# Fixing ScalarE's order, starting the weights' exponents a piece ahead, and moving loads to GpSimd's queue in a linear-attention and PReLU kernel

**Chip, cores, metric.** One core of one Trainium2 chip. Times are device microseconds (us) of one execution, the median of several runs; profile spans are a little shorter than the timed run (by about 2 us). All runs quoted were in the fast state and gave correct results.

Engines by their short names: PE (TensorE, matrix products), DVE (VectorE), ACT (ScalarE), GpSimd (POOL in the profile), SP (SyncE, here only an issuer of transfers).

## The reference

Gated linear attention over 768 positions, then a two-layer network with a PReLU between, all in float32. The weights arrive as float64, that is as pairs of 32-bit words, and are converted on the chip.

```python
f = 1.0 / (1.0 + np.exp(-f_logit))                    # (B=4, H=8, S=768, D=48)
for t in range(S):
    state = f[:, :, t, :, None] * state + np.einsum('bhd,bhe->bhde', k[:, :, t], v[:, :, t])
    y[:, :, t] = np.einsum('bhd,bhde->bhe', q[:, :, t], state)
x = y.transpose(0, 2, 1, 3).reshape(B * S, H * D)      # 3072 x 384
h = x @ w_in                                           # 384 x 2048
out = (np.maximum(h, 0) + alpha * np.minimum(h, 0)) @ w_out   # 2048 x 384
```

## The kernel before

The work is cut into 12 steps (6 chunks of 128 positions times 2 pairs of batches). A step interleaves the attention of one chunk with the network of the chunk before it. Both are Python generators; a string per step says in which order their pieces are emitted: P or Q are the seven preparation pieces (of this or of the next chunk), S the attention products, n the twelve network pieces (eight `ph` pairs, four `po`), w and v one piece each of the conversion of `w_in` and `w_out`. The first four steps have strings of their own, for there the conversion competes with everything else.

```python
def load_weights(dst, src, name):                      # pieces w and v
    for n in [...]:
        raw = work.tile([128, WP, 2], I32, tag="raw", ..., bufs=4)
        nc.sync.dma_start(out=raw..., in_=src[:, n:n + WP].bitcast(I32))
        lo, hi = raw[:, :, 0], raw[:, :, 1]
        e = work.tile([128, WP], I32, tag="e", ...)    # the pool's two buffers
        nc.vector.tensor_scalar(e, hi, 0x7FF00000, None, ALU.bitwise_and)
        nc.scalar.activation(e, e, AF.Relu, bias=bias, scale=8.0)      # the exponent, on ACT
        m = work.tile([128, WP], U32, tag="m", ...)
        nc.vector.tensor_scalar(m, ...)                # four more DVE instructions;
        nc.vector.scalar_tensor_tensor(m, ...)
        nc.vector.scalar_tensor_tensor(e, hi, ..., e, ...)   # this one waits for ACT
        nc.vector.scalar_tensor_tensor(flat[:, n:n + WP], m, 2.0 ** -31, e.bitcast(F32), ...)
        yield
...
# attention, from the states on                          # last piece S
        yield
        for ...: nc.scalar.copy(A[...], ad[...])
        for ...: nc.scalar.copy(A[...], off[...])
        py = pair(f"py_{i}")
        ...                                             # products into py
        y = work.tile([128, U, HP, C], F32, tag="y", ..., bufs=1)
        for u in range(U):
            nc.scalar.copy(y[:, u]..., py[:, u])        # ACT
        for hd in range(H):                             # ten transfers y -> xT
            ...
            (nc.sync if hd % 2 else nc.scalar).dma_start(out=xT[...], in_=y[...])
        yield
...
# network, last piece n
        for u in range(U):
            nc.scalar.copy(o, po[u][:, 0:DM])           # ACT, waits for the end of po
            nc.sync.dma_start(out=out[t0:t0 + C], in_=o)
        yield
...
    first = (
        "P7 S w S w S w S w S w2",
        "n w n w n w n w n w n w n2 P7 S v S v S v S v2 S v n2 v3 n v3 n",
        "n P n P n P n P n P n P n P n S n S n S2 n S Q3 n",
        "n P n P n P n P S n2 S n2 S n S n S Q4 n Q3 n",
    )
    with tc.manual_schedule(engines={mybir.EngineType.PE, mybir.EngineType.DVE}):
        ...
```

`manual_schedule` makes the program's order the order of the engines it names; on the others the scheduler chooses.

Names in the views: a chunk's attention goes from f (decay, after the sigmoid), kr, fs, qd and us (preparation) by `raw`, `qu`, `ad`, `off` and A (weights within the chunk) and ksn and `pd` (turned keys and increments of the state) to py, y and its rearranged form xT. The network goes from xT by `ph` (xT times `w_in`), neg (its negative part) and g (the PReLU, with om = 1 - alpha) to `po` (g times `w_out`) and its copy o.

Of the kernel before, what the change touches and what calls it, by code (L numbers as in the profile page):

```python
# [8 lines left out]
F32 = mybir.dt.float32  # L9
I32 = mybir.dt.int32  # L10
U32 = mybir.dt.uint32
AF = mybir.ActivationFunctionType
ALU = mybir.AluOpType

C = 128
DB = 32
MASKED = (1, 0)

U = 2
CH = 64  # L20
NC2 = C // CH
NB = DB // 4
WP = 512
# [3 lines left out]
def kernel(  # L27
# [28 lines left out]
    nc = tc.nc  # L56
    B, NC, _, HP, _ = qT.shape
    DM = v.shape[-1]
# [9 lines left out]
    NJ = C // DB  # L68
# [6 lines left out]
    work = ctx.enter_context(tc.tile_pool(name="work", bufs=2))  # L75
# [3 lines left out]
    def pair(name):  # L79
        return psa.tile([128, 2, 512], F32, tag="pair", name=name)  # L80
# [6 lines left out]
    om = const.tile([128, NF], F32, tag="om", name="om")  # L87
# [2 lines left out]
    lvl = const.tile([128, 2, DB], F32, tag="lvl", name="lvl")  # L90
    nc.scalar.dma_start(out=lvl, in_=masks)
    nc.scalar.dma_start(out=om, in_=alpha)
    nc.scalar.activation(om, om, AF.Identity, bias=1.0, scale=-1.0)



# [9 lines left out]
    for m in range(1, NB):  # L106
        lo = UO[m] + (4 if m == 1 else 0)
        n = NB - m
# [16 lines left out]
    bias = const.tile([128, 1], F32, tag="bias", name="bias")  # L125
    nc.gpsimd.memset(bias, -896.0 * 2.0 ** 23)
    ad = const.tile([128, U, 2, HP, DB], F32, tag="ad", name="ad")
    nc.gpsimd.memset(ad, 0.0)
    A = const.tile([128, U, H, C], F32, tag="A", name="A")
    nc.gpsimd.memset(A, 0.0)  # L130

    def load_weights(dst, src, name):





        flat = dst.rearrange("p a n -> p (a n)")
        ks = NK if dst is w_in_sb else 1
        per = flat.shape[1] // ks  # L140
        for n in [k * per + j for j in range(0, per, WP) for k in range(ks)]:
            raw = work.tile([128, WP, 2], I32, tag="raw", name=f"{name}_raw{n}", bufs=4)
            nc.sync.dma_start(out=raw.rearrange("p n two -> p (n two)"),
                              in_=src[:, n:n + WP].bitcast(I32))
            lo, hi = raw[:, :, 0], raw[:, :, 1]

            e = work.tile([128, WP], I32, tag="e", name=f"{name}_e{n}")
            nc.vector.tensor_scalar(e, hi, 0x7FF00000, None, ALU.bitwise_and)
            nc.scalar.activation(e, e, AF.Relu, bias=bias, scale=8.0)

            m = work.tile([128, WP], U32, tag="m", name=f"{name}_m{n}")
            nc.vector.tensor_scalar(m, hi.bitcast(U32), 11, 0x80000000, ALU.logical_shift_left, ALU.bitwise_or)
            nc.vector.scalar_tensor_tensor(m, lo.bitcast(U32), 21, m, ALU.logical_shift_right, ALU.bitwise_or)
            nc.vector.scalar_tensor_tensor(e, hi, -0x80000000, e, ALU.bitwise_and, ALU.bitwise_or)
            nc.vector.scalar_tensor_tensor(flat[:, n:n + WP], m, 2.0 ** -31, e.bitcast(F32), ALU.mult, ALU.mult)  # L155
            yield

    def rows(par):
        return slice(64 * par, 64 * par + D)

    def quads(t):
        return t.rearrange("p (n r) -> p n r", r=4)

    def attention(bp, c, x):

        i = f"{bp}_{c}"
        b0 = U * bp

        def load(name, src, bufs=2):
            t = work.tile([128, W], F32, tag=name, name=f"{name}_{i}", bufs=bufs)  # L170
            nc.sync.dma_start(out=t.rearrange("p (u x) -> p u x", u=U),
                              in_=src[b0:b0 + U, c].rearrange("u p h t -> p u (h t)"))
            return t

        f = quads(load("f", fT))
        q = load("q", qT, 1)
        k = load("k", kT)


# [27 lines left out]
        for m in range(2, NB):  # L207
            n = NB - m
# [16 lines left out]

        vt = work.tile([128, U, DM + 16], F32, tag="v", name=f"v_{i}", bufs=1)
        nc.gpsimd.memset(vt[:, :, DM:DM + 16], 0.0)
        nc.sync.dma_start(out=vt[:, :, 0:DM], in_=v[b0:b0 + U, c].rearrange("u t d -> t u d"))


        q3 = work.tile([128, GC, 3, DB], F32, tag="q3", name=f"q3_{i}", bufs=1)
# [20 lines left out]
        for u in range(U):  # L252
# [24 lines left out]
            for m in range(1, NB):  # L277
                lo = UO[m] + (4 if m == 1 else 0)
                n = DB - 4 * m
# [5 lines left out]
        off = pair(f"off_{i}")  # L285
        for u in range(U):
            for hp in range(HP):
                for cc in range(NC2):
                    g = (u * HP + hp) * NC2 + cc
                    o = (u * HP + hp) * DB  # L290
                    for par in range(2):
                        r_ = rows(par)
                        nc.tensor.matmul(off[CH * cc:CH * cc + DB, par, o:o + DB],  # L293
                                         lhsT=kh[r_, g], rhs=q3[r_, g, 2], start=True, stop=True)


        pk = pair(f"pk_{i}")
# [4 lines left out]
        ksn = work.tile([128, U, HP * 128], F32, tag="ksn", name=f"ksn_{i}", bufs=1)  # L302
        for u in range(U):
            nc.scalar.copy(ksn[:, u], pk[:, u])
        yield
        pd = pair(f"pd_{i}")
        for u in range(U):
            for hp in range(HP):
                for cc in range(NC2):
                    for par in range(2):  # L310
                        o = (u * HP + hp) * D
                        hd = 2 * hp + par
                        s_ = slice(CH * cc, CH * cc + CH)
# [17 lines left out]
        yield  # L331


        for j in range(NJ):
            s_ = slice(DB * j, DB * (j + 1))
            nc.scalar.copy(A[s_, :, :, s_], ad[s_].rearrange("p u r h t -> p u (r h) t"))  # L336
        for cc in range(NC2):
            s_ = slice(CH * cc, CH * cc + DB)
            for par in range(2):
                nc.scalar.copy(A[s_, :, par * HP:(par + 1) * HP, CH * cc + DB:CH * (cc + 1)],  # L340
                               off[s_, par, 0:U * HP * DB].rearrange("p (u h t) -> p u h t", u=U, h=HP))


        py = pair(f"py_{i}")
        for u in range(U):
            for hp in range(HP):
# [5 lines left out]
        for cc in range(NC2):  # L352
            if states[cc] is None:
                continue
            for u in range(U):
                for hp in range(HP):
                    for par in range(2):
                        r_ = rows(par)
                        o = hp * C + cc * CH
                        nc.tensor.matmul(py[64 * par:64 * par + D, u, o:o + CH],  # L360
                                         lhsT=states[cc][r_, u * HP + hp], rhs=qs[r_, u, hp, cc, 0:CH],
                                         start=False, stop=True, skip_group_check=True)
        y = work.tile([128, U, HP, C], F32, tag="y", name=f"y_{i}", bufs=1)
        for u in range(U):
            nc.scalar.copy(y[:, u].rearrange("p h t -> p (h t)"), py[:, u])
        xT = x["T"] = work.tile([128, NK, T], F32, tag="xT", name=f"xT_{i}")
        for hd in range(H):
            d = hd * D
            while d < (hd + 1) * D:
                n = min((hd + 1) * D, (d // 128 + 1) * 128) - d  # L370
                p0 = 64 * (hd % 2) + d - hd * D
                (nc.sync if hd % 2 else nc.scalar).dma_start(
                    out=xT[d % 128:d % 128 + n, d // 128].rearrange("p (u t) -> p u t", u=U),
                    in_=y[p0:p0 + n, :, hd // 2])
# [3 lines left out]
    def network(bp, c, x):  # L378
# [38 lines left out]
    steps = [(bp, c) for c in range(NC) for bp in range(B // U)]  # L417
    state = [None] * (B // U)
    first = (
        "P7 S w S w S w S w S w2",  # L420
        "n w n w n w n w n w n w n2 P7 S v S v S v S v2 S v n2 v3 n v3 n",
        "n P n P n P n P n P n P n P n S n S n S2 n S Q3 n",
        "n P n P n P n P S n2 S n2 S n S n S Q4 n Q3 n",
    )
    usual = "S n Q n S n Q n S Q n S Q n Q n S Q2 n5"
    pieces = {"w": load_weights(w_in_sb, w_in, "w_in"), "v": load_weights(w_out_sb, w_out, "w_out")}

    def begin(n):
        if n >= len(steps):
            return None, None  # L430
        x = {}
        return attention(*steps[n], x), network(*steps[n], x)

    with tc.manual_schedule(engines={mybir.EngineType.PE, mybir.EngineType.DVE}):
        att, net = begin(0)
        before = None
        for n in range(len(steps) + 1):
            coming, after = begin(n + 1)
            on = pieces | {"P": att, "S": att, "n": before, "Q": coming}
            for key in (first[n] if n < len(first) else usual).split():  # L440
                for _ in range(int(key[1:] or 1)):
                    if on[key[0]] is not None:
                        next(on[key[0]])
            before, att, net = net, coming, after
# [55 lines left out]
```

## Time and profile before

| | before |
|---|---|
| time, median of the first 3 runs | 736.37 us (734.86 to 737.44) |
| span of the profile | 732.2 us |
| start of step 2 (first `ph` of its network) | 152.83 us |
| `ph` of step 3's network flows (runs on without a long pause) from | 209.28 us |
| start of step 4 (`raw`), from here 52.57 us a step, PE never idle | 266.39 us |

The prediction shows the slices, the stretches and DVE's waits. Here are PE's own waits in the whole span. The columns are microseconds in total, how many waits, the longest.

```profile
PE raw L259 <- DVE qd L193: 18.9, 2, 13.1
...
PE po L402 <- DVE w_out_sb L155: 4.7, 4, 1.2
PE ph L386 <- DMA xT<-y: 4.2, 2, 4.0
...
PE pd L314 <- ACT ksn L304: 2.3, 3, 1.0
```

The line to remember is `ph <- DMA xT<-y`: the network of a chunk cannot begin before the ten transfers that turn y into xT have landed. Before the change that costs PE 4.2 us, nearly all of it once, in step 0, where there is no other network to work on meanwhile.

### The profile page before, as it was taken

How to read it: one execution, taken by the hardware profiler on the slowest of the kernel's cores; microseconds unless marked ns; L12 is line 12 of the kernel's file. 1: busy time of each engine (PE TensorE's matmuls, PEld its weight loads, DVE VectorE, ACT ScalarE, POOL GpSimd, SP SyncE). 2: the span in 40 equal slices, each digit the busy share in tenths (PEclk: the TensorE clock that was granted, in tenths of full speed). 3: DMA queues.
4: the chain of work that ended last, by engine and by line, in shares of the span. 5: the costliest groups of instructions: out<-in, count | busy, mean ns of one | idle time of the engine just before them, and what ended most of it. 6: DMA issues, size and time to landing. Idle time of an engine off the chain costs nothing.

```text
span 732.2 us, 17405 instructions
## 1 busy us (share of the span) xinstructions
PE 654.6 (89%) x7712; PEld 488.7 (67%) x7712; DVE 446.5 (61%) x895; ACT 187.2 (26%) x327; POOL 8.9 (1%) x42
## 2 busy tenths in 40 slices
PE   1368436889998999999999999999999999999997
PEld 0357335467677668678678678588687687687774
DVE  5969698869639588548458368279088186250020
ACT  3243114222222225114015024043041041041110
POOL 4000000000000000000000000000000000000000
PEclk9989855999999999999999999999999999999999
DMA  9244215401121022112121022022021001000000
GB/s 337 90 135 145 80 32 183 148 22 30 60 94 59 5 91 89 45 27 87 41 78 55 22 81 64 10 82 74 11 70 45 22 4 44 22 3 22 22 0 22
DMA packets 31466, 46.77 MB, mean 64 GB/s; under 512 B 3744, under 2 KB 19104, under 8 KB 31392
## 3 DMA queue, kind: packets, MB, share of 16 engines
q1 hardware_dynamic: 25536, 43.26, 18.7%
q10 hardware_dynamic: 5856, 2.40, 1.4%
q8 instruction: 61, 1.00, 0.6%
q14 instruction: 13, 0.11, 0.0%
HBM read 36.22 MB, written 4.72 MB: 56 GB/s over the span
## 4 chain that ended last, share of the span: by engine, by line
PE 78%; DVE 17%; ACT 2%; issue 1%; DMA 1%; ACTq 1%; DVEq 0%
PE ph L386 31%; PE po L402 31%; PE py L349 4%; PE py L360 3%; PE raw L259 2%; PE qu L275 2%; DVE us L210 2%; PE pk L301 2%; DVE ad L280 2%; PE pd L314 2%; DVE g L394 2%; DVE ad L266 1%; PE off L293 1%; DVE qd L193 1%; DVE w_out_sb L155 1%
## 5 line engine op out<-in xcount | busy, mean ns | idle before, releaser
L386 PE MATMUL ph<-xT,w_in_sb 128*128 128x256 f32 x1152 | 267.6, 389 | 13.0 <-DVE w_in_sb L155 8.0
L402 PE MATMUL po<-w_out_sb,g 128*128 128x384 f32 x768 | 252.6, 488 | 4.7 <-DVE w_out_sb L155 4.7
L386 PEld LDWEIGHTS ph<-xT,w_in_sb 128*128 128x128 f32 x1152 | 218.6, 193 | 50.4 <-DVE w_in_sb L155 9.4
L402 PEld LDWEIGHTS po<-w_out_sb,g 128*128 128x128 f32 x768 | 144.7, 190 | 105.1 <-DVE w_out_sb L155 8.5
L394 DVE SCALAR_TENSOR_TENSOR g<-neg,om,ph 128x256 f32<-128x256 f32 x192 | 83.2, 475 | 95.3 <-ACT neg L391 95.3
L266 DVE COPY_PREDICATED ad<-mraw,raw 128x256 f32<-128x256 int32 x96 | 42.5, 443 | 124.8 <-PE raw L259 122.3
L391 ACT ACTIVATE neg<-ph 128x512 f32<-128x512 f32 x96 | 57.1, 595 | 160.3 <-PE ph L386 128.2
L259 PE MATMUL raw<-qd,k 48*32 48x128 f32 x1536 | 31.0, 297 | 30.4 <-DVE qd L193 18.9
L408 ACT COPY o<-po 128x384 f32<-128x384 f32 x24 | 11.4, 480 | 172.0 <-PE po L402 172.0
L280 DVE COPY_PREDICATED ad<-mquad,qu 128x224 f32<-128x224 int32 (+6 forms) x168 | 50.3, 300 | 7.4
L259 PEld LDWEIGHTS raw<-qd,k 48*32 48x32 f32 x1536 | 23.9, 114 | 40.1 <-issue 35.7
L210 DVE TENSOR_TENSOR us<-us,fs 128x768 f32<-128x768 f32 (+2 forms) x72 | 44.9, 624 | 2.1
L275 PE MATMUL qu<-us,k 48*32 48x116 f32 x1536 | 29.3, 288 | 13.0 <-DVE us L210 9.9
L336 ACT COPY A<-ad 32x512 f32<-32x512 f32 x48 | 29.6, 616 | 35.5 <-DVE ad L280 34.9
L275 PEld LDWEIGHTS qu<-us,k 48*32 48x32 f32 x1536 | 23.9, 114 | 15.3 <-issue 7.0
L349 PE MATMUL py<-A,v 128*64 128x128 f32 x384 | 27.0, 300 | 2.4 <-issue 1.2
L349 PEld LDWEIGHTS py<-A,v 128*64 128x64 f32 x384 | 23.9, 152 | 6.4 <-issue 5.1
L193 DVE TENSOR_TENSOR qd<-qd,f 128x768 f32<-128x768 f32 (+2 forms) x36 | 27.3, 759 | 0.8
L199 DVE TENSOR_TENSOR us<-qd,f 128x1024 f32<-128x1024 f32 x12 | 24.1, 2009 | 0.1
L360 PE MATMUL py<-q,state 48*48 48x64 f32 x704 | 22.9, 221 | 0.0
L360 PEld LDWEIGHTS py<-q,state 48*48 48x48 f32 x704 | 21.1, 123 | 2.4 <-issue 2.4
L180 ACT ACTIVATE f<-f 128x1024 f32<-128x1024 f32 x12 | 12.7, 1057 | 36.1 <-DMA f<-in_fT 36.1
(62 smaller groups left out, 365.0 us busy)
## 6 DMA issues: line engine op xcount, KB each, us to landing
f<-in_fT SPq DMA_DIRECT2D x12, 512.0 KB, 3.8
q<-in_qT SPq DMA_DIRECT2D x12, 512.0 KB, 5.0
k<-in_kT SPq DMA_DIRECT2D x12, 512.0 KB, 3.9
w_in_raw<-in_w_in SPq DMA_DIRECT2D x12, 512.0 KB, 3.8
w_out_raw<-in_w_out SPq DMA_DIRECT2D x12, 512.0 KB, 3.5
v<-in_v SPq DMA_DIRECT2D x12, 384.0 KB, 3.3
out<-o SPq DMA_DIRECT2D x24, 192.0 KB, 2.0
xT<-y SPq DMA_DIRECT2D x36, 48.0 KB, 2.0
```

The costliest lines, as they stand in the source:

```text
L193: nc.vector.tensor_tensor(quads(qdv[d])[:, :, d:4], quads(qdv[d - 1])[:, :, d:4], f[:, :, 1:5 - d], ALU.mult)
L210: nc.vector.tensor_tensor(us[:, :, UO[m]:UO[m] + 4 * n].rearrange("p g (i r) -> p g i r", r=4), us[:, :, skip:skip + 4 * n].rearrange("p g ...
L259: nc.tensor.matmul(raw[DB * j:DB * (j + 1), par, hp * C:(hp + 1) * C], lhsT=k[r_, g:g + DB], rhs=qd[r_, 0:4 * W].rearrange("p (d x) -> p d ...
L266: nc.vector.copy_predicated(adu, mraw[:, d].rearrange("p i r -> p (i r)").bitcast(I32).unsqueeze(1).broadcast_to((128, H, DB)), rv[:, :, d])
L275: nc.tensor.matmul(qu[DB * j:DB * (j + 1), par, hp * UW:(hp + 1) * UW], lhsT=k4[r_, g * DB:(g + 1) * DB], rhs=us[r_, g], start=True, stop= ...
L280: nc.vector.copy_predicated(ad[:, u, :, :, 4 * m:DB], mquad[:, lo:lo + n].bitcast(I32).unsqueeze(1).unsqueeze(1).broadcast_to((128, 2, HP, ...
L349: nc.tensor.matmul(py[64 * par:64 * par + 64, u, hp * C:(hp + 1) * C], lhsT=vt[:, u, hd * D:hd * D + 64], rhs=A[:, u, par * HP + hp], star ...
L360: nc.tensor.matmul(py[64 * par:64 * par + D, u, o:o + CH], lhsT=states[cc][r_, u * HP + hp], rhs=qs[r_, u, hp, cc, 0:CH], start=False, sto ...
L386: nc.tensor.matmul(ph[:, j * T:(j + 1) * T], lhsT=w_in_sb[:, kt, (f + j) * 128:(f + j + 1) * 128], rhs=xT[:, kt], start=(kt == 0), stop=(k ...
L391: nc.scalar.activation(neg, phv, AF.Relu, scale=-1.0)
L394: nc.vector.scalar_tensor_tensor(g[:, j], neg[:, j], om[:, f + j:f + j + 1], phv[:, j], ALU.mult, ALU.add)
L402: nc.tensor.matmul(po[u][:, 0:DM], lhsT=gs[f // 2][:, f % 2, u * C:(u + 1) * C], rhs=w_out_sb[:, f], start=(f == 0), stop=(f == NF - 1))
```

## The change

Its intent, read from the code: ACT's exponent of a piece should be ready when DVE comes to use it; ACT should do things in an order chosen by hand; SP should have fewer loads to issue, so that xT is issued promptly; the orders of the first steps are tuned to this.

```diff
-    nc.scalar.activation(om, om, AF.Identity, bias=1.0, scale=-1.0)
+    nc.gpsimd.tensor_scalar(om, om, -1.0, 1.0, ALU.mult, ALU.add)
...
+        rest = None
         for n in [...]:
...
             nc.scalar.activation(e, e, AF.Relu, bias=bias, scale=8.0)
-            m = ...                     # the other four DVE instructions, at once
+            def finish(n=n, lo=lo, hi=hi, e=e):
+                m = ..., bufs=1         # the same four instructions
+            if rest is not None:
+                rest()
+            rest = finish
             yield
+        rest()
+        yield
...
+        loads = nc.gpsimd if bp or c else nc.sync      # q, k, f and v of all steps but the first
...
   # A's copies from off moved ahead of pk, those from ad ahead of the yield that precedes pd
...
+        yield                           # a new piece S: y and xT by themselves
         y = work.tile([128, U, HP, C], F32, tag="y", name=f"y_{i}", bufs=1)
...
     first = (
-        "P7 S w S w S w S w S w2",
-        "n w n w n w n w n w n w n2 P7 S v S v S v S v2 S v n2 v3 n v3 n",
-        "n P n P n P n P n P n P n P n S n S n S2 n S Q3 n",
-        "n P n P n P n P S n2 S n2 S n S n S Q4 n Q3 n",
+        "P7 w S w S w S w S w S w2 S",
+        "n w n w n w n w n w n w n P n P3 v P3 S v2 S v2 S v2 S v S v n v n S v n v2 n",
+        "n P n P n P n P n P n P n P n S n S n S2 n S Q3 n S",
+        "n P n P n P n P S n2 S n2 S n S n S Q4 n S Q3 n",
     )
-    usual = "S n Q n S n Q n S Q n S Q n Q n S Q2 n5"
+    usual = "S n Q n S n Q n S Q n S Q n Q n S Q2 n S n4"
...
-    with tc.manual_schedule(engines={mybir.EngineType.PE, mybir.EngineType.DVE}):
+    with tc.manual_schedule(engines={mybir.EngineType.PE, mybir.EngineType.DVE, mybir.EngineType.Activation}):
```

Two places deserve a look before reading on. In the first string the new last S (y and xT) stands behind `w2`; in the third it stands behind the last `n`, the piece that ends with the copies of o.

> **What bounds the kernel now.** I read first the page's slices, then busy time by stretch, then the timelines of single engines. The slices say that two kernels are glued together: a start in which VectorE (DVE) is busiest and TensorE (PE) often idle or at half clock, then a PE-bound rest.
>
> ```profile
> PE   1368436889998999999999999999999999999997
> DVE  5969698869639588548458368279088186250020
> PEclk9989855999999999999999999999999999999999
> ```
>
> The stretches, cut where PE begins the network of a step (`ph` or the attention pieces before it); columns are length, then busy time and count of PE, its weight loads, DVE, ScalarE (ACT), GpSimd, then clock, DMA:
>
> ```profile
> 0.00:152.83 152.83, 84.42 (x1073) 62.31 (x1074) 121.06 (x233) 45.59 (x70) 7.75 (x33) 0.84 0.43 138
> 152.83:207.81 54.98, 53.04 (x649) 39.48 (x648) 37.84 (x72) 14.88 (x26) 0.12 (x1) 1.00 0.19 59
> 207.81:266.46 58.65, 55.20 (x657) 40.52 (x662) 41.91 (x81) 14.97 (x27) 0.12 (x1) 0.97 0.17 51
> 266.46:319.03 52.57, 52.57 (x657) 39.51 (x663) 32.04 (x65) 13.74 (x25) 0.12 (x1) 1.00 0.19 54
> ```
>
> From 266.46 on PE never idles and each step takes 52.57 us. PE's own order is the same there after the change, so 732.2 - 266.46 = 465.7 us cannot move unless a load or ACT newly makes PE wait. Steps 2 and 3 can yield at most 2.4 + 6.1 us; the rest must come out of the first 152.8 us.
>
> The waits there (who waited, for whom: us, times, longest):
>
> ```profile
> DVE g L394 <- ACT neg L391: 31.1, 10, 11.3
> DVE w_in_e L154 <- ACT w_in_e L149: 5.3, 3, 4.1
> DVE kr L182 <- ACT f L180: 4.0, 1, 4.0
> DVE w_out_e L154 <- ACT w_out_e L149: 2.8, 2, 1.9
> ```
>
> The second and fourth are what "begun a piece ahead" is aimed at: 8.1 us. Moving `om` off ACT is aimed at the third. But most of the 5.3 us is one wait, inside the handover of the first step to its network:
>
> ```profile
> 47.23 1.07 ACT L365 COPY y<-py 128x512 f32<-128x512 f32 x2 [1.88 <-PE py L360]
> 48.34 3.39 ACTq L372 DMA_DIRECT2D xT<-y  x5
> 52.52 0.69 DVE L154 SCALAR_TENSOR_TENSOR w_in_e<-w_in_raw,w_in_e 128x512 int32<-128x512 int32 x1 [4.14 <-ACT w_in_e L149]
> 57.94 0.48 DVE L394 SCALAR_TENSOR_TENSOR g<-neg,om,ph 128x256 f32<-128x256 f32 x1 [1.26 <-ACT neg L391]
> ```
>
> DVE cannot pass `g` before y, its ten transfers xT, `ph` and `neg` are through; what it saves before, it waits there.
>
> **What the Trainium skill says.** "TensorE: Matmul & The Clock Gate", Architectural detail, calls ACT and DVE strict FIFO: an instruction that waits holds all behind it. The trace agrees: the issues of xT at 48.34 hold the exponent of that piece, hence the 4.14 us. The same page, Part 1, says an idle PE drops to half clock and needs some 3.4 us of work to return; the trace shows 0.50 in the stretch 95 to 125 us, and `ph` at 0.34 us a record in 79.7 to 86.5 us (20 in 6.85) against 0.217 (96 in 20.88). "Trainium Kernel Development and Optimization", Key Constraints, says that transfers of all queues share the same 16 engines, issuing from another saves only issue time; no slice after the first is near full (0.17 to 0.19 by step), so Pool's queue relieves nothing that binds. "ScalarE: Activation LUTs", What ACT_TABLE_LOAD costs, gives some 1283 ns for a table load (its head says 2.7 us); the trace has 1.283, twice; one of them goes.
>
> **The change part by part.** I lay the engines' new orders end to end with durations of the trace before: a weights piece 2.72 us on DVE (0.34 of it the exponent mask), an `ad` group 4.2, states 1.65, a pair of g 0.79, an exponent on ACT 0.7.
>
> (1) *`om` to GpSimd.* f was issued at 0.73 and lands some 4.1 later, so the sigmoid can start near 4.9 instead of 7.50: 2.6 us. But GpSimd now stands at om until 5.97, ahead of its whole chain of fills:
>
> ```profile
> 4.49 0.62 POOL L101 COPY mraw<-lvl 128x32 f32<-128x32 f32 x4 [3.10 <-DMA lvl<-in_masks]
> 8.12 0.40 POOL L121 MEMSET fs<- 128x289 f32 x1
> ```
>
> The chain moves from 4.49 to 6.1, fs is filled at 10.13 instead of 8.52, and DVE's write of fs, at 10.00 now, waits for it: about 10.2. Gain zero, loss 0.2.
>
> (2) *ACT's fixed order, step 0.* DVE: preparation ends 25.05, mask 25.4, `ad` 29.6, piece 32.3, `ad` 36.5, two pieces 41.95, states 43.6, two pieces 49.05, the mask of the seventh piece 49.4. The new ACT order has the seventh piece's exponent ahead of y: y starts at 50.1, not 47.23, though py is ready at 47.5. SyncE's queue has the tenth piece's load ahead of its half of xT; its buffer comes free at 51.05, and one of the xT transfers waits for that load's semaphore (55.05 with 4.0 us to landing), landing at 57.1. With PE cold, `ph` 0 then ends near 61.7, g at 62.3 instead of 57.94: 4.4 later, with the same six pieces done.
>
> (3) *The piece-ahead loop.* g at 62.35, then six g pairs, five pieces, and a last finish of 2.38: 4.74 + 13.6 + 2.38 = 20.7, the last w_in at 83.05 (before 79.61). `ph` 6 cold 3.9, `ph` 7 3.05, neg 0.6, then the qd copy on ACT: 91.65 instead of 89.85. Moving kr and fs into the gap gives back 1.9, the shorter tail 0.4: shift 1.8.
>
> (4) *Step 1.* 91.65 + 14.27 + 0.34 = 106.3; `ad` 110.5; two pieces 115.9; `ad` 120.1 (before 115.3); one piece and a mask 123.2, for the fifth w_out exponent stands ahead of the A copies on ACT: 123.9. off copies 1.27, ksn 1.1, A 2.5: 128.75. py 3.68 + 1.26: 133.7, before 126.03. DVE is through with w_out at 148.6 instead of 150.1, so `po` waits for it no longer, but 64 records at 0.3225 from 133.7 end at 154.4; before, 152.83. Shift 1.5: PE's late start takes what DVE gained.
>
> (5) *Step 2.* Same PE and DVE order, 54.98: `po` ends at 209.4. But here the new order puts y behind the last network piece, that is behind the copies of o, which wait for the end of `po`. Before, y ran in the middle of `po`:
>
> ```profile
> 202.54 1.07 ACT L365 COPY y<-py 128x512 f32<-128x512 f32 x2 [9.96 <-PE py L360]
> 208.47 0.86 ACT L408 COPY o<-po 128x384 f32<-128x384 f32 x2 [2.31 <-PE po L402]
> 207.81 0.70 PE L386 MATMUL ph<-xT,w_in_sb 128*128 128x256 f32 x2
> 209.28 6.09 PE L386 MATMUL ph<-xT,w_in_sb 128*128 128x256 f32 x26 [0.78 <-issue]
> ```
>
> PE's next work needs xT. So o 0.55, y 1.07, xT 2.84 to the first `ph` and 4.25 to the second (51.14 and 52.55 less 48.30): `ph` flows from 215.3, not 209.28. PE idles 4.5 us and then 0.7 more, goes cold, and the first two `ph` take 7.4 instead of 5.3: another 2.
>
> (6) *Step 3.* Its middle is DVE-bound behind the second g (waits of 1.41 and 1.26 us on `ad` now), so the delay passes through: 1.5 + 4.5 + 2 = 8 us at its end. Steps 4 to 11: y precedes the o copies again, xT has 20 us of `po` to land, loads are a step ahead: nothing. Sum +8, on 736.4: **744**.
>
> **The rivals.** *The gains are real:* 8.1 us of exponent waits and 2.6 at the head go, and I place the new waits wrongly: 725 to 728. For it, the orders look tuned; against, the 4.14 us and the g wait are one handover, and (5) stands in the listing of the new order without any estimate. *Steps 2 and 3 absorb it:* the pause lets DVE run ahead, the 2.67 us of `ad` waits and the cold 1.1 in 232 to 239 vanish: 739 to 740. Against, DVE's order in step 3 is tied to each g. *Loads bind:* GpSimd makes descriptors itself and its fills of v wait for py; if a load came late by 1 us in each of 12 steps: 756. Against, f has two buffers, and q is asked for a step ahead.
>
> **Range and chances.** The pause of (5) is the surest, 5 us; (2) to (4) may be 3 us off either way since each engine waits at several places; cold clock 2. Range 737 to 751. Over 2% faster needs below 721.6, beyond all removed waits together: 0.04. Over 2% slower needs above 751.1, late loads or cold clock beyond this: 0.10. Within 2%: 0.86.
>
> **What would show it.** fs on DVE waits for GpSimd near 10.2; y of step 0 starts near 50 behind an exponent; py of step 1 ends near 134, `po` has no w_out wait; PE idles about 5 us between step 2's `po` and the next `ph`, with y after o on ACT; 52.57 us steps unchanged. Wrong if that idle is under 2 us, if `po` of step 1 ends before 150, or if later steps grow beyond 52.6.

## The result

| | before | changed |
|---|---|---|
| median of 4 runs each, same rounds | 736.08 us | 743.34 us (741.74 to 746.11) |
| span of the profile | 732.2 us | 741.3 us |

The ratio is 1.0102, with a 95% interval from 1.0067 to 1.0138: slower by one per cent, within 2%. (All ratios and intervals are those on record, for fast runs against the kernel before in the same rounds, so not quite the ratios of the medians quoted. The kernel before ran again with each set of experiments: medians 735.98, 736.04 and 736.22 us.)

Slices of the changed kernel, in the same 40 parts as in the prediction:

```profile
PE   1448714999879999999999999999999999999998
...
DVE  5975799959518688818638548368188087151020
...
PEclk9987865899989999999999999999999999999999
```

PE's slice 3 is emptier than before (4 against 6), and a second cold spot, that is one of lower granted clock, appears at slice 12 (217 us on). The stretches, cut at the same events as before:

```profile
0.00:156.57 156.57, 82.86 (x1072) 62.69 (x1073) 121.72 (x233) 39.53 (x64) 15.92 (x44) 0.81 0.41 131
156.57:217.60 61.03, 53.79 (x652) 39.80 (x650) 38.04 (x72) 17.12 (x30) 4.39 (x7) 0.99 0.24 70
217.60:275.93 58.33, 55.65 (x647) 41.19 (x647) 41.83 (x81) 13.66 (x24) 2.94 (x5) 0.95 0.14 42
275.93:328.49 52.56, 52.56 (x650) 39.50 (x649) 31.99 (x65) 13.94 (x25) 3.01 (x5) 1.00 0.19 54
```

The second and third rows are cut where `ph` flows, so they are set against 152.83, 209.28 and 266.39 of the kernel before. Step 2 starts 3.74 us later. From there to flowing `ph` takes 61.03 instead of 56.45 us, 4.58 more; step 3 takes 58.33 instead of 57.11, 1.22 more. That makes 9.54 at the start of step 4; from there on the spans agree to 0.4 us. The loss thus has two places, before step 2 and at its end. PE's waits name them:

```profile
PE raw L269 <- DVE qd L203: 16.8, 2, 12.6
PE ph L396 <- DMA xT<-y: 15.3, 3, 10.1
...
PE pd L333 <- ACT ksn L319: 5.5, 3, 3.7
```

The wait for xT grew from 4.2 to 15.3 us and has a new place. The waits of `po` for `w_out` (4.7 us before) are gone from the list, as intended; in step 1 `pd` waits 3.67 us for ACT's ksn instead.

**Step 0's handover.** ACT's timeline (start, length, instruction, idle time ahead of it and what ended it), then PE's:

```profile
49.09 0.72 ACT L150 ACTIVATE w_in_e<-w_in_e,bias 128x512 int32<-128x512 int32 x1 [2.12 <-DVE w_in_e L149]
49.72 1.05 ACT L375 COPY y<-py 128x512 f32<-128x512 f32 x2
50.80 3.49 ACTq L382 DMA_DIRECT2D xT<-y  x5
```

```profile
56.88 2.41 PE L396 MATMUL ph<-xT,w_in_sb 128*128 128x256 f32 x4 [10.10 <-DMA xT<-y]
59.48 12.48 PE L396 MATMUL ph<-xT,w_in_sb 128*128 128x256 f32 x48 [0.19 <-issue]
```

The copy of y shows no idle time ahead of it, which can mislead: ACT idled 2.12 us in front of the *exponent*, and py had been ready since 46.78. y waited 2.9 us behind an instruction that has nothing to do with it. The ten transfers are then slow too, as SP's timeline and the view of the xT tile in this stretch tell:

```profile
40.67 10.41 SPq L144 DMA_DIRECT2D w_in_raw<-in_w_in  x4
51.17 6.86 SPq L382 DMA_DIRECT2D xT<-y  x5
```

```profile
DMA to landing us min/median/max: 1.8/4.7/5.5
```

(Landing is counted from issue until the data has arrived.) Before, the same line read 1.9/2.1/2.4. Now loads of weights of 512 KB each are under way when the xT transfers of 16 to 48 KB are issued (the DMA share is 0.86 from 46 to 50 and 0.75 from 50 to 54 us; before, 0.70 and 0.35). The last of these loads goes out at 50.75, just ahead of the first xT, and lands at 56.10; that xT, issued at 50.80, lands at 56.34. SP's third xT issue waits 3.4 us, to 56.12, until that load has landed, so that the last one goes out at 57.4 us. From the start of y to flowing `ph` it is 59.48 - 49.72 = 9.8 us, against 52.55 - 47.23 = 5.3 before.

**Step 2's handover.** ACT:

```profile
211.07 0.48 ACT L418 COPY o<-po 128x384 f32<-128x384 f32 x1 [9.56 <-PE po L412]
211.72 0.48 ACT L418 COPY o<-po 128x384 f32<-128x384 f32 x1 [0.17 <-PE po L412]
212.09 1.08 ACT L375 COPY y<-py 128x512 f32<-128x512 f32 x2
```

and PE:

```profile
206.25 5.43 PE L412 MATMUL po<-w_out_sb,g 128*128 128x384 f32 x16
216.05 0.70 PE L396 MATMUL ph<-xT,w_in_sb 128*128 128x256 f32 x2 [4.37 <-DMA xT<-y]
217.60 13.19 PE L396 MATMUL ph<-xT,w_in_sb 128*128 128x256 f32 x46 [0.85 <-DMA xT<-y]
```

py was ready at 206.3, and ACT idled 9.56 us in front of o, which needs the end of `po`. Only then comes y. PE stands still 4.37 and 0.85 us, and the next 6.4 us run at a granted clock of 0.52.

### The profile page after: what moved, and what is told of

It reads as the page before. It is cut to its first block, busy times and chain, and to the rows that moved or that the text cites. A ratio compares the mean times of both kernels' runs of the same rounds, so it can differ in the third digit from the quotient of the medians.

```text
span 741.3 us, 17451 instructions
## 1 busy us (share of the span) xinstructions
PE 654.2 (88%) x7712; PEld 490.1 (66%) x7712; DVE 447.1 (60%) x895; ACT 186.3 (25%) x325; POOL 41.4 (6%) x87
## 2 busy tenths in 40 slices
DMA packets 25483, 46.78 MB, mean 63 GB/s; under 512 B 3744, under 2 KB 16464, under 8 KB 25408
## 4 chain that ended last, share of the span: by engine, by line
PE 77%; DVE 17%; ACT 2%; issue 2%; DMA 1%; POOL 1%; ACTq 0%; DVEq 0%; POOLq 0%
PE po L412 33%; PE ph L396 30%; PE py L358 3%; PE py L369 3%; PE raw L269 2%; PE qu L285 2%; DVE us L220 2%; DVE ad L290 2%; DVE g L404 2%; PE pd L333 1%; DVE ad L276 1%; PE pk L316 1%; DVE w_in_m L156 1%; DMA xT<-y 1%; PE off L303 1%
## 5 line engine op out<-in xcount | busy, mean ns | idle before, releaser
L396 PE MATMUL ph<-xT,w_in_sb 128*128 128x256 f32 x1152 | 270.2, 392 | 22.6 <-DMA xT<-y 15.3
L285 PE MATMUL qu<-us,k 48*32 48x116 f32 x1536 | 28.7, 284 | 14.2 <-DVE us L220 10.9
L181 POOL DMA_DIRECT2D k<-in_kT x11 | 8.0, 727 | 258.5 <-PE raw L269 258.5
```

What stands on the lines that cost most here:

```text
L285: nc.tensor.matmul(qu[DB * j:DB * (j + 1), par, hp * UW:(hp + 1) * UW], lhsT=k4[r_, g * DB:(g + 1) * DB], rhs=us[r_, g], start=True, stop= ...
L396: nc.tensor.matmul(ph[:, j * T:(j + 1) * T], lhsT=w_in_sb[:, kt, (f + j) * 128:(f + j + 1) * 128], rhs=xT[:, kt], start=(kt == 0), stop=(k ...
```

## The experiments

**Theory.** Two pieces in ACT's new fixed order cost the time: y behind the last exponent in step 0, and y behind o in step 2. Without them the change would gain. **Rivals.** (a) A program-fixed order on ACT is worse as such, since the scheduler fits ACT's small jobs into gaps. (b) Loads from GpSimd's queue are slower or disturb others. (c) `om` on GpSimd delays the start. (d) Starting exponents ahead costs DVE or ACT more than it saves. Experiments 1 to 6 edit the changed kernel; the later ones edit a run before them, as their texts say.

### 1. y ahead of o

```diff
-        "... S n S n S2 n S Q3 n S",
+        "... S n S n S2 n S2 Q3 n",
```

> The changed kernel with one word of step 2's order moved: y and xT are copied right after py, ahead of the last network piece and so of the o copies. My theory (y stands behind the o copies on ScalarE): TensorE's wait for xT at the start of step 3 (5.2 us in two pieces) falls below 1 us, ph stays at full clock there, the profiled span falls from 741.3 to about 734 and the time by 7 us to about 736. Rival (xT is late because of the transfers or the loads on GpSimd's queue): the wait stays above 3 us and the time above 741.

Measured: 739.32 us, ratio 1.0054 (1.0033 to 1.0075), 4 us gained instead of 7. The pause of PE is gone altogether: `po` ends at 210.8 and `ph` flows from 210.83. But DVE has a new wait; its waits from 190 to 275 us:

```profile
DVE kr L192 <- ACT f L190: 13.2, 1, 13.2
```

and ACT's timeline says why:

```profile
205.68 1.07 ACT L375 COPY y<-py 128x512 f32<-128x512 f32 x2 [7.58 <-PE py L369]
206.78 3.50 ACTq L382 DMA_DIRECT2D xT<-y  x5
210.33 1.06 ACT L190 ACTIVATE f<-f 128x1024 f32<-128x1024 f32 x1 [3.58 <-issue]
```

The next chunk's sigmoid, first piece of `Q3`, now stands behind y and its five issues. DVE cannot prepare the next chunk, and step 3 grew from 58.3 to 61.1 us (210.83 to 271.95). The pause was rightly named, but my repair made the same mistake in small: I had put something behind y without asking when y becomes ready. The next try puts y between the two.

### 2. y between the sigmoid and o

```diff
-        "... S n S n S2 n S Q3 n S",
+        "... S n S n S2 n S Q3 S n",
```

> The changed kernel with step 2's y and xT between the next step's first preparation (sigmoid, kr, qd) and the last network piece: y still ahead of the o copies, but the sigmoid not behind y, as it was in y_ahead_of_o, where VectorE then waited 13.2 us for it. My theory: no pause of TensorE at step 3 and no wait of VectorE for the sigmoid; from the end of step 2's po to the first raw of step 4 about 58.0 us (changed kernel 64.3, y_ahead_of_o 61.1, before 58.6); time 736.5 to 737.5. Rival (step 3 is bound by VectorE whatever y does): 61 us or more there, time 739 or more.

Measured: 736.00 us, ratio 1.0008 (0.9986 to 1.0029): 7.3 us off the changed kernel's 743.34, as much as its whole net loss. PE at the same place:

```profile
205.82 5.43 PE L412 MATMUL po<-w_out_sb,g 128*128 128x384 f32 x16
212.80 0.67 PE L396 MATMUL ph<-xT,w_in_sb 128*128 128x256 f32 x2 [1.55 <-DMA xT<-y]
213.74 10.47 PE L396 MATMUL ph<-xT,w_in_sb 128*128 128x256 f32 x46 [0.27 <-DMA xT<-y]
```

The pause is 1.55 and 0.27 us, where I had expected none. y is in time (205.94), but its transfers took 4.6 us to land by median, against 2.0 in run 1: the first, issued at 207.04, landed just behind GpSimd's load of v (issued at 206.83, landed at 211.74). So rival (b) is not empty: read from these landings, not tested by itself, a load issued right ahead of xT holds it up here, as SP's weight load does in step 0. The 46 records take 10.47 us instead of 13.19, at a granted clock of 1.00: PE did not go cold. Step 3 takes 55.6 us (213.74 to 269.35) where it took 58.3, so the pause's cost was not only its own length.

### 3. y of step 0 ahead of the last weights

```diff
-        "P7 w S w S w S w S w S w2 S",
+        "P7 w S w S w S w S w S2 w2",
```

> The changed kernel with step 0's last piece (y and xT) two weight pieces earlier, so y stands behind the fifth exponent instead of the seventh, and two weight loads go behind xT in SyncE's queue. My theory: y starts near 46.8 instead of 49.7, the first g at about 58 instead of 63.9, all later work of the first three steps moves by 5 to 6 us, time 737 to 738. Rival (VectorE's weights set this part whatever y does): the first g moves, but the last w_in and w_out pieces move by less than 2 us, time 741 or more.

Measured: 736.53 us, ratio 1.0009 (0.9983 to 1.0035), 6.8 us off. ACT and PE at the handover:

```profile
47.85 1.07 ACT L375 COPY y<-py 128x512 f32<-128x512 f32 x2 [2.24 <-PE py L369]
```

```profile
53.28 2.05 PE L396 MATMUL ph<-xT,w_in_sb 128*128 128x256 f32 x4 [5.47 <-DMA xT<-y]
55.66 10.54 PE L396 MATMUL ph<-xT,w_in_sb 128*128 128x256 f32 x45 [0.34 <-DMA xT<-y]
```

y starts at 47.85 us, right behind py, `ph` at 53.28 instead of 56.88, and step 2's network at 150.43 instead of 156.57. The edit moved two things at once, y on ACT and two loads to behind xT on SP. In the profiles y's place is worth 2.9 us (y now starts 0.04 us after py, not 2.94), and from the start of y to flowing `ph` it is 7.8 us instead of 9.8; no run parts the two. The pause at the end of step 2 is still there, 4.37 us, as in the changed kernel: the two faults are separate.

### 4. Both moves

> The changed kernel with only the two misplaced pieces moved, y0_early and y_between together. My theory: the two waits are independent and add up, 743.3 - 6.8 - 7.3 = 729.2, within 2 us, so that the changed kernel was slower for these two places alone. Rival (they hide behind each other, or the fixed order of ScalarE costs elsewhere too): 733 or more.

Edit: 2 and 3 together. Measured: 729.08 us, ratio 0.9902 (0.9867 to 0.9938). 743.34 less 729.08 is 14.3; the single moves gave 7.3 and 6.8. They add up. This kernel still has everything else of the change, ACT's fixed order, GpSimd's loads, `om` on GpSimd, and it is one per cent faster than the kernel before. So the rest of the change is worth some 7 us, and the two misplaced pieces cost 14.

### 5. ACT's order left to the scheduler

```diff
-    with tc.manual_schedule(engines={..PE, ..DVE, ..Activation}):
+    with tc.manual_schedule(engines={..PE, ..DVE}):
```

> The changed kernel with ScalarE given back to the scheduler, all else as changed (lookahead, om and loads on GpSimd, orders of TensorE and VectorE). My theory (both new waits are places in ScalarE's fixed order): y of step 0 and of step 2 go early again, the time falls by 9 to 13 us, to 730 to 734. Rival (loads on GpSimd or the new orders of TensorE and VectorE cost the time): it stays at 741 to 744.

Measured: 731.03 us, ratio 0.9934 (0.9906 to 0.9963), 12.3 us off. ACT and PE at step 0's handover:

```profile
46.75 0.59 ACT L375 COPY y<-py 128x512 f32<-128x512 f32 x1 [3.66 <-PE py L369]
47.23 0.72 ACT L150 ACTIVATE w_in_e<-w_in_e,bias 128x512 int32<-128x512 int32 x1
47.85 0.58 ACT L375 COPY y<-py 128x512 f32<-128x512 f32 x1
```

```profile
51.29 1.19 PE L396 MATMUL ph<-xT,w_in_sb 128*128 128x256 f32 x2 [4.59 <-DMA xT<-y]
52.77 12.32 PE L396 MATMUL ph<-xT,w_in_sb 128*128 128x256 f32 x50 [0.28 <-DMA xT<-y]
```

With the same strings the scheduler puts y where it is ready. The xT transfers land in 2.0 us (median), with a DMA share of 0.35 and 0.53 from 46 to 50 and 50 to 54 us. This run by itself fits rival (a) as well as the theory; run 4 decides, for there the order is fixed by the program and the time is no worse (729.08). Rival (a) falls.

### 6. `om` behind GpSimd's fills

Edit: the line `nc.gpsimd.tensor_scalar(om, ...)` moved behind `nc.gpsimd.memset(A, 0.0)`.

> The changed kernel with GpSimd's operation on om put behind its fills instead of ahead of them. My theory: VectorE's wait for the fill of fs (2.55 us) shrinks by 1.6 us since the chain of fills starts at the landing of lvl (3.2) and not of om (4.8); everything to the end of step 1 is 1.6 us earlier, time about 741.7. Rival (this head is hidden behind something later): no change, 743.3.

Measured: 742.10 us, ratio 1.0090 (1.0061 to 1.0118), 1.2 us below the changed kernel, with intervals that overlap: too small to be told from nothing. In the changed kernel's own profile the wait that I had foreseen at the start is there; GpSimd and DVE:

```profile
4.80 0.19 POOL L93 TENSOR_SCALAR om<-om 128x16 f32<-128x16 f32 x1 [3.39 <-DMA om<-in_alpha]
...
9.07 0.40 POOL L121 MEMSET fs<- 128x289 f32 x1
```

```profile
9.50 0.62 DVE L196 TENSOR_TENSOR fs<-f,kr 128x256 f32<-128x256 f32 x1 [2.55 <-POOL fs L121]
```

How much it costs depends on when two small transfers land: the table of masks landed at 3.20 us in that profile and at 4.40 in this run's, without any change to it. Here the write of fs came at 9.41, hardly earlier. Rival (c) can explain a microsecond, not seven.

### 7 and 8. No piece ahead; loads on SP, each with ACT free

```diff
-            if rest is not None:
-                rest()
-            rest = finish
+            finish()
```

> act_free (731.0) with each weights piece finished at once, as before the change. My theory: the lookahead was worth little, since most of the wait it removes sat in the handover to the network, and it costs 0.12 us a piece on VectorE; 729 to 734, and VectorE shows 1 to 6 us of waits for exponents. Rival (the lookahead is what makes act_free faster than the kernel before): 735 to 739.

```diff
-        loads = nc.gpsimd if bp or c else nc.sync
+        loads = nc.sync
```

> act_free (731.0) with all loads back on SyncE's queue. My theory: the transfers [...]were never late, so steps from the fourth on stay at 52.6 us and the time is within 3 us of 731. Rival (the loads on GpSimd are what makes act_free faster, or they cost something that this gives back): 735 or more, or 727 or less.

Measured: 731.58 us (ratio 0.9953, 0.9932 to 0.9974) without the piece ahead, 730.34 us (0.9944, 0.9915 to 0.9973) with all loads on SP; both beside 731.03 with them. Where ACT is free, neither part moves the time by anything these intervals can tell. The steps from 4 on are the same, and PE is busy 400 of the 400 us from 300 to 700 with loads on either queue. Without the piece ahead DVE waits 3.4 us for exponents, within the 1 to 6 expected. Rivals (b) and (d) fall as far as these two runs reach (neither part was undone with ACT's order fixed, and run 2 shows (b) at one place), and so does the part of the intent that rested on them. That fits the prediction's argument that what DVE saves ahead of a handover it waits at g; it was not shown piece by piece. What carries the gain was not isolated: the two parts were never undone together, and the new strings, the separate y piece, the copies of A and `om` were not parted from each other.

### 9. Better orders

> act_free with three buffers for the exponents (0.12 us a piece back on VectorE), om behind the fills, and step 1's weight pieces moved behind its states so that py and po start earlier. My theory: head 1.5 us earlier, w_out done 3 us earlier, po of step 1 starts near 122 and ends with w_out near 146 instead of 150: time 725 to 727. Rival (po keeps its place behind xT or the cold clock): 729 to 731.

> two_moves with the three further edits of free_best (three buffers for exponents, om behind the fills, step 1's pieces behind its states), ScalarE's order fixed. My theory: a fixed order is no cost in itself once its places are right, so it is within 2 us of free_best (727.0). Rival (ScalarE does better with the scheduler's order): 730 or more.

> free_best with GpSimd's fills (qd, kr, fs, ones, bias, ad, A) put ahead of its copies from lvl, which wait for a transfer. My theory: VectorE's wait for the fill of fs, still 2.3 us in om_late, goes wholly, and the 2 us pass through to the end since VectorE sets this part: 724.5 to 725.5. Rival (the handover to the network takes it back): 726.5 or more.

Edits: to `act_free` (free) or to run 4 (fixed) three more were added: `om` late, three buffers for the masks e (`bufs=3`), and a string for step 1 that puts fewer weights between the attention pieces:

```diff
-        "... P3 v P3 S v2 S v2 S v2 S v S v n v n S v n v2 n",
+        "... P3 v P3 S v S v S v S v2 S v2 n v n S v n v3 n",
```

`free_best2` also puts GpSimd's fills ahead of the copies that need the table of masks.

| | median us | ratio (95%) |
|---|---|---|
| free_best | 727.02 | 0.9892 (0.9868 to 0.9915) |
| fixed_best | 726.92 | 0.9868 (0.9833 to 0.9904) |
| free_best2 | 728.36 | 0.9883 (0.9856 to 0.9911) |

Free and fixed again agree, as expected; 727.02 is at the edge of the 725 to 727 expected of `free_best`. The third buffer answers something I had not foreseen: with two, a piece's mask is written into the buffer that the previous piece's last instruction has just read, and DVE pauses some 0.12 us; a piece takes 2.85 instead of 2.72 us where pieces follow each other directly. With three it takes 2.72 again. In step 1 of `fixed_best`, `pd` waits 0.82 us for ksn instead of 3.67, and `po` begins at 123.45 instead of 127.97 (run 4). PE then waits for `w_out` again:

```profile
141.53 1.56 PE L412 MATMUL po<-w_out_sb,g 128*128 128x384 f32 x4 [1.04 <-DVE w_out_sb L158]
144.05 2.85 PE L412 MATMUL po<-w_out_sb,g 128*128 128x384 f32 x8 [0.96 <-DVE w_out_sb L158]
```

So at the end of that stretch the conversion on DVE is the bound; whether a still better order would gain there was not tried.

`free_best2` missed: 724.5 to 725.5 was expected. GpSimd in it:

```profile
8.74 0.89 POOL L179 DMA_DIRECT2D f<-in_fT  x1
9.63 5.38 POOL L126 COPY mquad<-inq 128x28 f32<-128x28 f32 x7
14.96 0.72 POOL L179 DMA_DIRECT2D q<-in_qT  x1
```

These seven small copies took 1.01 us in `free_best`, where they ran from 4.09 us on with DVE idle. Moved later they run beside DVE's products of two tensors and take 5.38 us, and the issues of q and k wait behind them (14.96 instead of 11.04 us). The write of fs came no earlier (7.17 against 7.21 us, in a `free_best` profile whose mask table happened to land early, at 2.88 us). The difference between the two profiles lies in step 1, which took 97.7 us from flowing `ph` on, against 94.5; the granted clock differs by 0.09 at most (0.77 against 0.86 in the first 19 us), and the cause stays open. Their timed intervals overlap, so I take from this run only that it did not help, and the copies' slowdown.

The best ratio of all is that of `fixed_best`: 1.3% faster than the kernel before, with the change's own idea, the two pieces where they should stand, and three further edits.

## Why the prediction was right

744.0 was predicted, 743.34 measured, within the 2% to which it gave a chance of 0.86. By the prediction's steps:

- **(1) `om`.** Right in kind: fs waits for GpSimd. 10.2 predicted, 9.50 in the profile; the difference is the earlier landing of the two small transfers. The sigmoid's gain was indeed lost.
- **(2) Step 0's handover.** The mechanism held: y behind the seventh exponent, at 49.72 (50.1 predicted). The size was short. `ph` flowed at 59.48, not at 57.1, and g came at 63.91, not at 62.3. The mis-sized term is "one of the xT transfers waits for that load's semaphore (55.05 with 4.0 us to landing), landing at 57.1". The load did go out in time (50.75), but it took 5.4 us and landed at 56.10, and behind it stood not one but three of SP's xT issues, 0.65 us apart, the last of which landed at 59.39. That no DMA slice is near full was true of slices of 18 us; in the 4 us before the handover the share was 0.70.
- **(3) The loop.** DVE started on qd at 93.82, 91.65 predicted: the 1.6 of (2), and the rest because the last two `ph` were slower (20 records in 7.44 us instead of 6.85). From the first g to the last piece the estimate held: 20.8 us, 20.7 predicted.
- **(4) Step 1.** "`po` waits for it no longer" held; py ended at 135.9 (133.7 predicted), `po` at 156.57 (154.4). That the fifth `w_out` exponent delays ksn was right (`pd` waited 3.67 us). The shift at step 2 was 3.7 instead of 1.5; all of the 2.2 too little was inherited from (2) and (3), though DVE finished `w_out` at 152.05, not 148.6.
- **(5) The pause.** 4.5 and 0.7 us predicted, 4.37 and 0.85 measured. The cold clock was seen.
- **(6) Step 3.** "The delay passes through" held: +9.5 at its end in the profile, 8 predicted; the surplus is (2)'s, less 0.8 since step 3 lost 1.2 instead of 2. Later steps: 52.56 us, unchanged.

The sum was 8 us, the timed difference 7.3, the profiles' difference 9.1. So part of the close hit is luck: the undersized handover is 2 us, runs of the kernel before spread over 2.6 us, and its profiled run (733.96) was 2.4 below their median.

Two slips changed nothing in the sum. The first of the lines on DVE's waits (g: 31.1 us, 10, 11.3) is for the first 320 us, not for the 152.8 that the text names; up to 160 us it is 14.2, 4, 6.2. And in (3) the savings named, 1.9 and 0.4 off 4.4, would leave 2.1; the 1.8 used is what the chain of times gives.

The rival "the gains are real" was wrong as a forecast, yet the experiments show what it saw: with the two pieces moved the kernel reaches 729.1, and with three edits more, which are not part of the change, 726.9, inside its 725 to 728. "Loads bind" was wrong: the later steps took 52.56 us. "Steps 2 and 3 absorb it" was wrong as well: removing the pause gave 7.3 us, more than the pause itself.

## What to carry to other kernels

When an engine's order is fixed by hand, ask of each instruction what stands directly ahead of it on that engine and what *that* waits for; a copy that feeds the bound engine's next work must not stand behind an instruction that waits for the end of its present work, nor behind another engine's side job. In the profile, look for the idle time in front of the instruction *before* the late one. And test an order by moving one piece at a time: here two strings with one letter out of place hid a gain of one per cent, and the first repair of one of them moved the fault to its neighbour.

## What the Trainium skill lacked or had wrong

- "DMA: Bandwidth & Descriptors": its section Anatomy of one DMA fits a transfer, measured there for issues from GpSimd, by 2.0 us plus bytes over 436 GB/s. With no load issued right ahead, the xT transfers of 16 to 48 KB, issued from SP and ACT, agree (2.1 us median before, 2.0 with ACT free). Issued right behind a weight load they took 4.7 us in the changed kernel's step 0, and the page has no number for a small transfer that meets bulk loads. Loads of 512 KB took 3.4 to 5.7 us by median where the fit gives 3.2. For an issue from GpSimd instead of SP the page has some 0.4 us more to the first byte; the load of v (384 KB) took 3.3 us from SP and 3.6 to 4.5 from GpSimd, those of f (512 KB) 3.7 or 3.8 and 4.1 or 4.2. GpSimd itself was busy 0.72 to 0.89 us with each such issue, a number that the page lacks.
- "GPSIMD Engine Reference", Specifications, says that its memory interfaces are shared with VectorE and contended where a DVE instruction has two inputs there. The runs agree and add a size: seven copies of 128x28 or less took 1.01 us beside an idle DVE and 5.38 us beside DVE's two-tensor products. A fill of 128x2048, which reads nothing, took 1.8 us either way.
- The head of "ScalarE: Activation LUTs" has 2.7 us, which its section What ACT_TABLE_LOAD costs makes up of the load and some 1380 ns of drain. In the kernel before, the load between `om` and the sigmoid took 1.283 us, and from the end of `om` (6.18) to the sigmoid (7.50) it was 1.32 us in all: no such drain shows there.
- On no page that I read: DVE pauses some 0.12 us where an instruction writes a buffer that the one just ahead of it reads (a weights piece took 2.85 us with the mask buffer reused at once, 2.72 before).
